# Loading x ahead of the states, and compacting batch 2's x on GpSimd, at the start of a fused attention and maxout kernel

## The chip, the cores and the metric

One core of one Trainium2 chip. The metric is the device time of one execution in microseconds, outputs checked against the reference. Ratios are the mean time of one kernel's fast runs over that of the other's in the same rounds, so they differ a little from the ratio of the medians quoted. Short names: PE is TensorE, ACT is ScalarE, DVE is VectorE, POOL is GpSimd, SP is the engine that issues nearly all DMAs.

## The reference

```python
# x: (8 batches, 8 heads, 512, 64); state: (8, 8, 32, 64); w1, w2: (512, 1024); w_out: (1024, 512)
a     = softmax(x @ state.T / 8);   xread = a @ state
a2    = softmax(state @ x.T / 8);   sread = a2 @ x
y     = concat([xread, sread], axis=2)          # then heads side by side: 4352 x 512
out   = maximum(y @ w1, y @ w2) @ w_out
```

The kernel writes the maximum as relu(y (W1 - W2)) + y W2, so that it needs `wcat` = [W1 - W2 | W2 Wo] beside Wo, and multiplies the small state matrices by `wcat` once per batch (`u_sw`) instead of every row of xread. The result, copied ("evicted") from PSUM to SBUF by ACT and DVE, is `swt`; `l1` multiplies the attention by it, and the relu of that is `r`.

## The kernel before

One in-order program per engine. Weights are prepared while they are loaded; then batch 0 runs, interleaved with the start of batch 1; from batch 1 on a loop repeats, with PE as its bound. Each batch needs its x three ways: as f32 (`xf`), packed to bf16 (`xc`), from which a DMA makes the transpose `xt` that the scores (`u_exp`) read, and padded (`xp`), for the products that give sread. The parts that the change touches (cuts are marked):

```python
    load_states(first)                      # SP's program, in order
    load_x(0, 2)
    # ... W2, Wo in parts
    load_w(w1f, moe_w1, 0)                  # W1a: columns 0 to 511, 1 MB
    load_w(w1f, moe_w1, 1)                  # W1b
    load_states(second)                     # batches 1, 2
    load_x(1)
    load_states(rest)                       # batches 3 to 7
    load_x(2)
    # ...
    for e, i in (("V", slice(0, 2)), ("A", slice(2, 3)), ("P", slice(3, 4))):
        copy(e, w1b[:, i, 0:512], w1f[:, i, 0:512])        # V is DVE, A is ACT, P is POOL
    # ... last products of W2 Wo, their evictions
    u_sw(0, 0)
    u_sw(0, 2)
    w_sub(0); w_sub(1)                      # W1a - W2a on POOL
    l1(0, {}, range(0, 4))
    w_sub(2, nc.vector); w_sub(3, nc.vector)   # W1b - W2b on DVE
    compact_x(1, 0); compact_x(1, 1)        # xc of batch 1, on ACT
    d_xt(1)                                 # SP: transpose of xc into xt
    cast_states("P", second)
    cast_states("P", rest)
    cast_x(1)                               # xp of batch 1, on POOL
    load_x(3)
    sT = d_states(rest)
    # ... batch 0's output products, states(second) on PE, u_sw(0, 1), l1(0, 4..7), u_sw(1, 0)
    u_exp(1, 0); u_exp(1, 1)                # scores of batch 1: read xt
    # ...
    l2_close(0, 1)
    compact_x(2, 0); compact_x(2, 1)        # xc of batch 2, on ACT, one buffer for all batches
    d_xt(2)
    # ... the rest of batch 0, then the loop; in it u_exp(2, ...)
```

The softmax here doesn't subtract the row's maximum and nothing guards it: scores larger than these inputs give would overflow.

## Time and profile before

| | before |
|---|---|
| time, median | 151.57 us (151.40 to 151.83) |
| span of the profiled execution | 149.5 us |
| PE busy | 140.1 us, 94% |
| DMA's share of the chain that ended last | 16% |
| waits of PE for `xt`, batches 1 and 2, in brackets | 0.80 and 0.66 us |

The page's busy shares say that PE is the bound on average; they do not say where a microsecond can be had. That takes the chain in order of time and PE's own timeline, which the prediction shows. A timeline line is start, duration, engine, line, operation, count, and in brackets the idle time of the engine before it and what ended it.

The transpose of the states keeps SP for 4.55 us. Batch 2's `xt` is issued only at 40.62, when ACT has packed its x.

### The profile page before, as it was taken

To read this page: it belongs to the slowest core of one execution; us is meant where nothing else is said; L and a number is where in the kernel's file an instruction comes from. 1 tells how busy PE (TensorE), PEld (TensorE's weight loads), DVE (VectorE), ACT (ScalarE), POOL (GpSimd) and SP (SyncE) were. 2 spreads that over 40 slices of the span, in tenths; PEclk is the share of its full clock that TensorE was granted. 3 is DMA by queue.
4 is the path that set the end of the run, shared out by engine and by line. 5 is a ranking of instruction groups with operands and counts; after the bars stand their busy time and mean duration, and the time that the engine had idled before them with its cause. 6 is when DMAs were issued, how large, how long until landed. Compare 5 with 4: busy or idle time off the path is not lost.

```text
span 149.5 us, 2995 instructions
## 1 busy us (share of the span) xinstructions
PE 140.1 (94%) x1228; PEld 67.7 (45%) x1249; DVE 81.7 (55%) x150; ACT 74.9 (50%) x126; POOL 45.3 (30%) x47
## 2 busy tenths in 40 slices
PE   6988989997989999999999999999999999999991
PEld 2454633434435445444543454445445434664460
DVE  5338628967887097716754582658067725731120
ACT  3166437546877157626844683478157136521010
POOL 3144349880943330550064017104100500000000
PEclk9999999999999999999999999999999999999999
DMA  3999999989989967973979397851556030502423
GB/s 68 381 386 386 388 380 329 301 159 196 214 175 292 324 125 250 313 149 67 302 261 203 116 299 213 158 226 57 105 110 281 0 75 35 245 0 70 136 95 126
DMA packets 37966, 29.89 MB, mean 200 GB/s; under 512 B 24896, under 2 KB 33344, under 8 KB 37056
## 3 DMA queue, kind: packets, MB, share of 16 engines
q1 hardware_dynamic: 37808, 29.56, 69.5%
q8 instruction: 10, 0.16, 0.4%
q10 hardware_dynamic: 144, 0.13, 0.3%
q14 instruction: 4, 0.03, 0.1%
HBM read 15.20 MB, written 8.91 MB: 161 GB/s over the span
## 4 chain that ended last, share of the span: by engine, by line
PE 73%; DMA 16%; SPq 3%; DVE 2%; issue 2%; ACT 2%
PE acc L322 33%; PE ps L307 15%; DMA w1f<-in_moe_w_dram 10%; PE acc L318 9%; DMA xt<-xc 6%; PE ps L279 2%; PE ps L215 2%; PE ps L366 2%; PE acc L376 2%; SPq L98 2%; PE ps L238 2%; PE acc L356 1%; ACT xc L61 1%; PE acc L374 1%; PE acc L279 1%
## 5 line engine op out<-in xcount | busy, mean ns | idle before, releaser
L322 PE MATMUL acc<-wo,r 128*128 128x512 bf16 x238 | 58.3, 379 | 0.5
L322 PEld LDWEIGHTS <-r 128*128 128x128 bf16 x248 | 23.9, 98 | 28.3 <-issue 0.2
L225 POOL TENSOR_TENSOR a<-e,er 128x512 bf16<-128x512 bf16 x14 | 14.4, 1050 | 54.8 <-ACT e L218 39.1
L297 DVE TENSOR_SCALAR r<-ps 128x512 bf16<-128x512 f32 x32 | 22.1, 692 | 13.6 <-PE ps L307 13.6
L307 PE MATMUL ps<-aT,swt 128*128 128x512 bf16 x127 | 29.1, 379 | 0.3 <-DVE swt L63 0.3
L63 DVE COPY ob<-acc 128x512 f32<-128x512 f32 (+1 forms) x17 | 11.1, 655 | 30.2 <-PE acc L322 29.8
L61 ACT COPY ob<-acc 128x512 f32<-128x512 f32 (+1 forms) x16 | 9.2, 574 | 28.6 <-PE acc L322 21.0
L295 ACT ACTIVATE r<-ps 128x512 bf16<-128x512 f32 x32 | 19.2, 602 | 5.9 <-PE ps L307 5.3
L307 PEld LDWEIGHTS <-swt 128*128 128x128 bf16 x128 | 12.1, 98 | 14.9 <-DVE swt L63 0.9
L318 PE MATMUL acc<-swt,aT 128*128 128x512 bf16 x56 | 16.7, 380 | 0.8 <-issue 0.8
L65 POOL CAST xp<-xf 128x2048 bf16<-128x2048 f32 (+1 forms) x8 | 14.1, 1762 | 9.6 <-DMA xf<-in_x_dram 9.6
L61 ACT CAST swt<-ps 128x512 bf16<-128x512 f32 x18 | 9.9, 588 | 13.8 <-PE ps L279 13.8
L61 ACT CAST xc<-xf 128x1024 bf16<-128x1024 f32 x14 | 13.9, 1050 | 1.7 <-DMA xf<-in_x_dram 1.7
L222 DVE TENSOR_REDUCE es<-e 128x16 f32<-128x512 bf16 x16 | 10.6, 659 | 5.0 <-ACT e L218 5.0
L63 DVE CAST swt<-ps 128x512 bf16<-128x512 f32 x18 | 11.6, 679 | 0.9 <-PE ps L279 0.9
L130 PE MATMUL ps<-warm 128*128 128x512 bf16 x24 | 8.7, 493 | 1.3 <-POOL warm L116 1.3
L218 ACT ACTIVATE e<-ps 128x512 bf16<-128x512 f32 x16 | 8.8, 595 | 2.1 <-PE ps L215 1.5
L411 PE MATMUL acc<-wo,w2t 128*128 128x512 bf16 x30 | 7.3, 379 | 0.1
L318 PEld LDWEIGHTS <-aT 128*128 128x128 bf16 x62 | 4.7, 97 | 6.0 <-issue 2.6
L215 PE MATMUL ps<-sbd,xt 128*128 128x64 bf16 x128 | 5.2, 193 | 2.0 <-DMA xt<-xc 1.5
L215 PEld LDWEIGHTS <-xt 128*128 128x128 bf16 x128 | 4.6, 98 | 4.4 <-DMA xt<-xc 2.3
L279 PE MATMUL ps<-wcat,sbd 64*32 64x512 bf16 x136 | 6.3, 382 | 0.0
(73 smaller groups left out, 116.0 us busy)
## 6 DMA issues: line engine op xcount, KB each, us to landing
xf<-in_x_dram SPq DMA_DIRECT2D x7, 1024.0 KB, 7.6
out_dram<-ob SPq DMA_DIRECT2D x7, 1024.0 KB, 5.0
w2f<-in_moe_w_dram SPq DMA_DIRECT2D x2, 1024.0 KB, 9.1
wof<-in_moe_w_out_dram SPq DMA_DIRECT2D x4, 512.0 KB, 10.3
w1f<-in_moe_w_dram SPq DMA_DIRECT2D x2, 1024.0 KB, 15.5
xf<-in_x_dram SPq DMA_DIRECT2D x2, 512.0 KB, 4.5
out_dram<-ob SPq DMA_DIRECT2D x3, 256.0 KB, 2.2
out_dram<-obs SPq DMA_DIRECT2D x8, 64.0 KB, 1.7
```

The lines of the kernel that those rows point to most:

```text
L61: nc.scalar.copy(o, i)
L63: nc.vector.tensor_copy(o, i)
L65: nc.gpsimd.tensor_copy(o, i)
L215: nc.tensor.matmul(p[:, k * 64:k * 64 + 64], d["xt"][:, 4 * i + 2 * g + cp, :], sbd[:, b, 2 * i + g].rearrange("p u n -> p (u n)"), start= ...
L222: nc.vector.tensor_reduce(d["es"][:, g], d["e"][:, g].rearrange("p i c n -> p (i c) n"), axis=mybir.AxisListType.X, op=ALU.add)
L225: mul.tensor_mul(d["a"][:, g].rearrange("p c i n -> p i c n"), d["e"][:, g], d["er"][:, g].rearrange("p (i c) -> p i c", i=4).unsqueeze(3) ...
L279: nc.tensor.matmul(pg[g][32 * i:32 * i + 32, :], sneg[gs, i, :] if k else sbd[gs, b, 2 * i + g, g, :], w[gs, i, ch * 512:(ch + 1) * 512], ...
L295: nc.scalar.activation(out=o, in_=p, func=ACTF.Relu)
L297: nc.vector.tensor_scalar(o, p, scalar1=0.0, scalar2=None, op0=ALU.max)
L307: nc.tensor.matmul(p, SW[b][:, g, f * 128:(f + 1) * 128], AT[b][:, g, :], start=(g == 0), stop=(g == 1))
L318: nc.tensor.matmul(OB[b][1 + c], AT[b][:, g, c * 128:(c + 1) * 128], SW[b][:, g, FF:WC], start=(g == 0), stop=False)
L322: nc.tensor.matmul(OB[b][1 + c], R[b][:, f, c * 128:(c + 1) * 128], wo[:, f, :], start=False, stop=(f == NF - 1))
```

## The change

It means to have x on the chip earlier: x1 (the x of batch 1) ahead of the states of batches 1 and 2, x2 ahead of the other states, batch 2's packing on an idle engine as soon as x2 has landed, into a second buffer, and W1a in two loads, so that half of its casts is done before the rest lands. To make room for that, batch 1's `xp` cast goes from POOL to ACT, and the cast and transpose of the other states come later.

```diff
-            st[b]["xc"] = at.tile([128, H, NC * D], BF16, tag="xc", bufs=1, name="xc")
+            st[b]["xc"] = at.tile([128, H, NC * D], BF16, tag="xc", name="xc")      # pool's two buffers
...
-    load_w(w1f, moe_w1, 0)
+    load_w(w1f, moe_w1, 0, 2)              # two DMAs of half the rows' blocks
     load_w(w1f, moe_w1, 1)
+    load_x(1)
     load_states(second)
-    load_x(1)
-    load_states(rest)
     load_x(2)
...
-    for e, i in (("V", slice(0, 2)), ("A", slice(2, 3)), ("P", slice(3, 4))):
+    for e, i in (("P", slice(0, 1)), ("A", slice(1, 2)), ("V", slice(2, 3)), ("A", slice(3, 4))):
...
     d_xt(1)
+    load_states(rest)
+    cast_x(1, (("A", slice(0, 4)), ("A", slice(4, 8))))
     cast_states("P", second)
-    cast_states("P", rest)
-    cast_x(1)
+    compact_x(2, 0, "P")
+    compact_x(2, 1, "P")
+    d_xt(2)
     load_x(3)
-    sT = d_states(rest)
...
     u_norm(1, 1, nc.gpsimd)
+    cast_states("P", rest)
+    sT = d_states(rest)
     cast_x(2)
...
     l2_close(0, 1)
-    compact_x(2, 0)
-    compact_x(2, 1)
-    d_xt(2)
```

More of the change, by code (lines that the diff above doesn't have):

```diff
@@ L91, with load_w @@
     wof = stage.tile([128, NF, DM], F32)
-    def load_w(t, w, ch):
+    def load_w(t, w, ch, parts=1):
         cs = slice(ch * 512, (ch + 1) * 512)
-        nc.sync.dma_start(out=t[:, :, cs], in_=w.rearrange("(i p) f -> p i f", p=128)[:, :, cs])
+        for k in range(parts):
+            i = slice(4 * k // parts, 4 * (k + 1) // parts)
+            nc.sync.dma_start(out=t[:, i, cs], in_=w.rearrange("(i p) f -> p i f", p=128)[:, i, cs])
     def load_wo(q):
```

## The prediction

> **What bounds the kernel now.** I read the page of the profile first: who is busy, and the chain that ended last.
>
> ```profile
> PE 140.1 (94%) x1228; PEld 67.7 (45%) x1249; DVE 81.7 (55%) x150; ACT 74.9 (50%) x126; POOL 45.3 (30%) x47
> ...
> PE 73%; DMA 16%; SPq 3%; DVE 2%; issue 2%; ACT 2%
> PE acc L322 33%; PE ps L307 15%; DMA w1f<-in_moe_w_dram 10%; PE acc L318 9%; DMA xt<-xc 6%; PE ps L279 2%; PE ps L215 2%; PE ps L366 2%; PE acc L376 2%; SPq L98 2%; PE ps L238 2%; PE acc L356 1%; ACT xc L61 1%; PE acc L374 1%; PE acc L279 1%
> ```
>
> The tensor engine (PE) is busy for 94% of a 149.5 us span and the chain runs through it for 73%. Only two transfers stand in the chain in bulk: the load of W1 (10%) and the transposes of x (6%). The change aims at both. The chain of waits in order of time places them.
>
> ```profile
> 6.24 15.41 DMA w1f<-in_moe_w_dram
> 21.65 0.02 issue
> 21.68 0.69 DVE w1b L63
> ...
> 30.07 4.78 DMA xt<-xc
> 34.85 0.05 issue
> 34.90 0.66 PE ps L215 x16
> ...
> 38.60 1.99 ACT xc L61 x2
> 40.59 0.03 ACT swt L61
> 40.62 4.30 DMA xt<-xc
> 44.92 0.04 issue
> 44.96 0.64 PE ps L215 x16
> ```
>
> Columns are start, duration, what. After 45.0 us the chain has nothing but PE, with pauses of 0.05 to 0.2 us, so nothing that the change does can gain there. Transposes of batches 1 and 2 are each waited for. But a chain counts the whole transfer, and the price is the idle time of PE, which its timeline shows in brackets.
>
> ```profile
> 22.42 0.86 PE L279 MATMUL ps<-w1b,sbd 64*32 64x512 bf16 x8 [0.35 <-DVE w1b L63]
> 22.90 0.60 PE L279 MATMUL ps<-w2b,sneg 64*32 64x512 bf16 x8
> 23.13 0.88 PE L279 MATMUL ps<-wcat,sbd 64*32 64x512 bf16 x8
> 24.27 1.90 PE L307 MATMUL ps<-aT,swt 128*128 128x512 bf16 x8 [0.26 <-DVE swt L63]
> ...
> 34.90 0.64 PE L215 MATMUL ps<-sbd,xt 128*128 128x64 bf16 x16 [0.80 <-DMA xt<-xc]
> ...
> 44.96 0.64 PE L215 MATMUL ps<-sbd,xt 128*128 128x64 bf16 x16 [0.66 <-DMA xt<-xc]
> ```
>
> Open gaps: 0.35 + 0.26 + 0.80 + 0.66 = 2.07 us. Two hidden ones: eight L279 matmuls take 0.41 us later in the trace (at 30.64) and 0.86 and 0.88 here, some 0.45 us lost each. All of it, about 3.0 us, is 2% of the time: the **ceiling** of this change.
>
> **What the Trainium skill says.** "SBUF — State Buffer", section "Who interferes with whom", says that GpSimd (POOL) and VectorE (DVE) share one pair of ports as an exclusive lock: a DVE copy or cast in a two-port mode, or a DVE instruction with two SBUF inputs, fully blocks a GpSimd read, or is blocked, by who issues first. The trace agrees:
>
> ```profile
> 21.70 1.14 POOL L65 CAST w1b<-w1f 128x512 bf16<-128x512 f32 x1 [1.68 <-DMA w1f<-in_moe_w_dram]
> 22.81 4.67 POOL L385 TENSOR_TENSOR wcat<-w1f,w2f 128x1024 bf16<-128x1024 f32 x2
> 27.42 1.61 POOL L65 CAST s_bf<-s_f 128x512 bf16<-128x512 f32 x1
> ```
>
> 512 elements took 1.61 us beside the DVE subtraction of 26.81 to 30.1, although 1280 took 1.76 and 1024 mostly 1.04. The w1b cast of 512 took 1.14, and ended 0.47 us after the DVE cast that started with it (21.68 + 0.69 = 22.37). "GPSIMD Engine Reference", section "4.1 Engine selection", calls one-input GpSimd work "roughly line-rate". The trace: 1024 elements to bf16 took 1.04 us on POOL and 1.05 on ScalarE (ACT), so moving the compaction costs nothing. "DMA: Bandwidth & Descriptors", section "Why small descriptors are slow (HBM only)", gives 256-byte pieces a fixed cost. States go in such pieces: by the landing records the 320 KB of batches 3 to 7 stood 1.38 us behind batch 1's x (28.03 to 29.41), 237 GB/s, while the 1 MB of W1b took 2.82 us (21.65 to 24.47), 372 GB/s.
>
> **The change part by part.**
>
> *W1a in two.* Wo's last part lands at 18.93 and W1a at 21.65, so the first half should land near 20.3. POOL and ACT are free by then (their casts and copies end at 20.0 and 19.3) and finish slices 0 and 1 before 21.65. Then DVE casts one slice (0.43 by its 512-element casts, was 0.69 for two) to 22.1 and ACT one (0.62) to 22.3. PE finishes its previous matmuls at 22.08. The last slice was ready at 22.84 on POOL, so L279 has its inputs 0.54 us earlier. But wcat needs ACT's two copies (to 23.27) and DVE's two (end 23.57, now near 23.3), so L307 starts near 24.0 instead of 24.27: **0.27 us gained**. POOL's two subtractions start up to 0.7 us earlier.
>
> *Order of loads.* x1 takes 3.06 us and the states of batches 1 and 2 take 0.50 (landings 24.97, 28.03). Swapped: x1 lands at 27.5 instead of 28.03, those states at 28.0 instead of 24.97. x2 loses the 1.38 us of the other states ahead of it: 31.2 instead of 32.55.
>
> *The states now come late.* POOL's cast starts at 28.0, behind DVE's subtractions (to about 29.0), and takes 0.6: ready at 29.6. PE arrives at its transposes (29.46 before) near 29.2: a **new stall of 0.4 us**. In addition ACT, after compacting x1 (27.5 to 29.5), now casts x1 too: 2 x 1.05, to 31.6, and only then evicts its half of swt (to 32.2; was 31.74). The L307 of 31.86 moves to about 32.2, and PE reaches batch 1's scores near 34.2 (34.1 before, when it then waited to 34.90).
>
> *xt of batch 1.* Issued at 29.55 rather than 30.07; 4.3 to 4.8 us to landing gives 33.9 to 34.3. Scores start near 34.25: **0.65 earlier in all**, with the 0.27 above already in it, because this wait swallows PE's small delays.
>
> *xt of batch 2.* Its compaction stood in ACT's program behind an output copy, at 38.6, though x2 had landed at 32.55. Now POOL does it at 31.2 to 33.3, its transpose is issued at 33.3 and lands by 38.5, five microseconds before PE asks (about 43.6). The **0.66 us** go.
>
> *What is put off.* The 320 KB of states, their cast (behind POOL's products, to about 39.6) and transpose come later: that transpose is issued over 4.55 us, 39.6 to 44.2 (33.74 before). Its reader was at 55.0, so it is hidden, but the output of batch 0 and the load of x4 behind it go some 0.7 us later, and batch 3's xt, landed at 56.63 for a use at 58.94, may land near 57.4 for a use at 57.6: **0 to 0.5 us back, I take 0.2**.
>
> Sum: 0.65 + 0.66 - 0.2 = 1.1 us; 151.57 - 1.1 = 150.5.
>
> **Rivals.** (1) *The lock turns on PE's path.* At W1a's landing DVE's slice cast and POOL's subtraction start on the same event. If POOL is first, DVE waits out 2.36 us and u_sw of batch 0 is some 2 us late; batch 1's wait can absorb 0.65 of it and batch 2's gap still closes: about 152.4. Before, DVE was 0.03 us ahead of POOL on that event, so I give this one in seven. (2) *A late state replaces the late x.* If the states land at 29 and the cast meets the subtraction, PE stalls 1.4 us at the state transposes; only batch 2's gap is won: 150.9. For it: POOL, PE and DVE meet in this microsecond. (3) *The delayed queue eats it.* If batch 3's xt or its a-transpose is late by a microsecond, it is 151.3 or no gain. Against it: the slack of 2.3 us. (4) *All goes well*, hidden L279 losses included: 149.5.
>
> **Range and chances.** Two gaps worth 1.3 us are nearly sure to shrink; the rest are exchanges of some tenths. Low 149.7 is nearly all of the gaps; high 152.0 takes in rivals 2 and 3 and part of 1. Faster by 2% (under 148.5) would need 3.0 us, the whole ceiling: 3%. Slower by 2% (over 154.6) would need rival 1 with another stall: 4%. Within: 93%.
>
> **What would show it.** L215's two bracketed waits should be gone or under 0.2 us; xc of batch 2 on POOL near 31 to 33.3; x2's landing near 31.2. A wait of about 0.4 before the state transposes (L154) at 29 to 30 shows the swap's price. L307's first group at 24.0 shows the W1a split; at 26 it shows rival 1, with DVE's w1b cast over 2 us long. A bracketed wait before batch 3's L215 near 57.6 shows rival 3. The prediction is wrong if a wait that I don't have appears on PE after 45 us, or if a POOL cast runs into the products that PE's a-transposes of batch 1 need at 39.2.

## More of the kernel before

One more view is needed later: how SP issued the transposes before. The columns are start, duration of the issue on SP, queue, line, what.

```profile
30.07 3.00 SPq L189 DMA_TRANSPOSE xt<-xc  x1
33.19 0.50 SPq L80 DMA_DIRECT2D xf<-in_x_dram  x1
33.74 4.55 SPq L142 DMA_TRANSPOSE sT<-s_bf  x1
40.62 2.82 SPq L189 DMA_TRANSPOSE xt<-xc  x1
43.55 0.52 SPq L332 DMA_DIRECT2D out_dram<-ob  x1
```

## The result, and the profile after

The changed kernel took **149.73 us** (149.66 to 149.82, 4 runs) against 151.49 for the kernel before in the same rounds: ratio 0.9881, 95% interval 0.9863 to 0.9899. A later set of rounds, `e11` below, gave 149.75 and 0.9898 (0.9882 to 0.9915). So the gain is 1.5 to 1.8 us where 1.1 was forecast.

The page of the kernel after, its chain by engine and line:

```profile
PE 74%; DMA 14%; SPq 7%; ACT 2%; issue 1%
PE acc L323 34%; PE ps L308 16%; DMA xf<-in_x_dram 11%; PE acc L319 8%; SPq L97 4%; DMA xt<-xc 3%; PE ps L280 3%; PE ps L216 2%; PE ps L367 2%; PE acc L377 2%; PE ps L239 2%; SPq L100 2%; PE acc L357 1%; ACT xc L61 1%; PE acc L375 1%
```

`xt` has gone from 6% to 3%: one transpose is left of two. The load of W1 has been replaced by the load of x (`xf`). The chain in order of time, for the kernel after, says which transpose is left:

```profile
11.39 16.16 DMA xf<-in_x_dram
27.57 1.99 ACT xc L61 x2
29.59 4.50 DMA xt<-xc
```

It is batch 1's: x1 lands, ACT packs it, the DMA transposes it, PE starts. PE's timeline after, at the places that the prediction showed for before (lines are one higher than before: L216 was L215):

```profile
23.92 1.90 PE L308 MATMUL ps<-aT,swt 128*128 128x512 bf16 x8 [0.21 <-DVE swt L63]
...
29.34 0.40 PE L155 MATMUL ps<-ident,s_bf 128*128 128x128 bf16 x4
...
33.61 0.41 PE L280 MATMUL ps<-wcat,sbd 64*32 64x512 bf16 x8
34.14 0.71 PE L216 MATMUL ps<-sbd,xt 128*128 128x64 bf16 x16
...
40.01 3.63 PE L308 MATMUL ps<-aT,swt 128*128 128x512 bf16 x16
43.47 0.63 PE L216 MATMUL ps<-sbd,xt 128*128 128x64 bf16 x16
...
57.43 0.63 PE L216 MATMUL ps<-sbd,xt 128*128 128x64 bf16 x16
```

Both bracketed waits are gone, though a little of the first is left: 0.53 us pass from the group ahead of batch 1's scores (33.61 to 34.14), where 0.34 do in `e9` below, whose `xt` is early. So 0.19 us are still waited; before, it was 0.87 (33.69 to 34.90, less 0.34). Set beside before:

| PE comes to | before, us | after, us | earlier by |
|---|---|---|---|
| first group of `l1` of batch 0 | 24.27 | 23.92 | 0.35 |
| scores of batch 1 | 34.90 | 34.14 | 0.76 |
| scores of batch 2 | 44.96 | 43.47 | 1.49 |
| scores of batch 3 | 58.94 | 57.43 | 1.51 |

After batch 2 nothing is won or lost. SP's issues and POOL's work after:

```profile
29.59 1.88 SPq L190 DMA_TRANSPOSE xt<-xc  x1
31.52 1.14 SPq L85 DMA_DIRECT2D s_f<-in_state_dram  x1
33.09 2.75 SPq L190 DMA_TRANSPOSE xt<-xc  x1
35.96 0.51 SPq L80 DMA_DIRECT2D xf<-in_x_dram  x1
39.64 1.51 SPq L143 DMA_TRANSPOSE sT<-s_bf  x1
41.24 1.20 SPq L333 DMA_DIRECT2D out_dram<-ob  x1
```

```profile
21.69 4.90 POOL L386 TENSOR_TENSOR wcat<-w1f,w2f 128x1024 bf16<-128x1024 f32 x2 [0.76 <-DMA w1f<-in_moe_w_dram]
...
28.16 1.13 POOL L65 CAST s_bf<-s_f 128x512 bf16<-128x512 f32 x1 [1.39 <-DMA s_f<-in_state_dram]
31.04 2.03 POOL L65 CAST xc<-xf 128x1024 bf16<-128x1024 f32 x2 [1.75 <-DMA xf<-in_x_dram]
36.36 2.06 POOL L226 TENSOR_TENSOR a<-e,er 128x512 bf16<-128x512 bf16 x2 [3.29 <-DVE er L225]
```

POOL packs batch 2's x at 31.04 in a hole that it had, and its transpose is issued at 33.09 instead of 40.62. The states' transpose, moved from 33.74 to 39.64, now takes 1.51 us to issue, not 4.55, and batch 0's output goes out at 41.24, 2.3 us *earlier* than before.

### The profile page after: what moved, and what is told of

Its sections match the earlier page's. It is cut to its first block, busy times and chain, and to the rows that moved or that the text cites. A ratio compares the mean times of both kernels' runs of the same rounds, so it can differ in the third digit from the quotient of the medians.

```text
span 147.9 us, 3003 instructions
## 1 busy us (share of the span) xinstructions
PE 139.4 (94%) x1228; PEld 67.4 (46%) x1249; DVE 81.7 (55%) x150; ACT 75.7 (51%) x127; POOL 44.2 (30%) x48
## 4 chain that ended last, share of the span: by engine, by line
PE 74%; DMA 14%; SPq 7%; ACT 2%; issue 1%
PE acc L323 34%; PE ps L308 16%; DMA xf<-in_x_dram 11%; PE acc L319 8%; SPq L97 4%; DMA xt<-xc 3%; PE ps L280 3%; PE ps L216 2%; PE ps L367 2%; PE acc L377 2%; PE ps L239 2%; SPq L100 2%; PE acc L357 1%; ACT xc L61 1%; PE acc L375 1%
## 5 line engine op out<-in xcount | busy, mean ns | idle before, releaser
L308 PE MATMUL ps<-aT,swt 128*128 128x512 bf16 x127 | 29.1, 379 | 0.3 <-DVE swt L63 0.2
L308 PEld LDWEIGHTS <-swt 128*128 128x128 bf16 x128 | 12.0, 98 | 15.0 <-DVE swt L63 0.8
L65 POOL CAST xp<-xf 128x2048 bf16<-128x2048 f32 (+1 forms) x7 | 12.2, 1745 | 11.0 <-DMA xf<-in_x_dram 11.0
L61 ACT CAST xc<-xf 128x1024 bf16<-128x1024 f32 x12 | 11.9, 1051 | 1.6 <-DMA xf<-in_x_dram 1.6
L131 PE MATMUL ps<-warm 128*128 128x512 bf16 x24 | 7.7, 444 | 1.3 <-POOL warm L117 1.3
L216 PEld LDWEIGHTS <-xt 128*128 128x128 bf16 x128 | 4.8, 98 | 2.8 <-ACT xt L61 0.8
L216 PE MATMUL ps<-sbd,xt 128*128 128x64 bf16 x128 | 5.3, 193 | 0.7 <-ACT xt L61 0.6
```

The lines of the kernel that those rows point to most:

```text
L61: nc.scalar.copy(o, i)
L65: nc.gpsimd.tensor_copy(o, i)
L216: nc.tensor.matmul(p[:, k * 64:k * 64 + 64], d["xt"][:, 4 * i + 2 * g + cp, :], sbd[:, b, 2 * i + g].rearrange("p u n -> p (u n)"), start= ...
L308: nc.tensor.matmul(p, SW[b][:, g, f * 128:(f + 1) * 128], AT[b][:, g, :], start=(g == 0), stop=(g == 1))
```

## The experiments

Twelve runs in three sets (`e11` is the changed kernel again); those of a set share the runs of the kernel before (medians 151.40, 151.33 and 151.48). "Worth" is one minus the ratio, times that median. All results were correct.

### One part alone

**`e1`: W1a's two loads and its casts, alone.**

```diff
-    load_w(w1f, moe_w1, 0)
+    load_w(w1f, moe_w1, 0, 2)
...    # and the changed kernel's tuple of casts
```

> The kernel before with only W1a's two loads and the new split of its casts. Theory A (the early part is bounded by batch 1's xt, which lands at 34.85 whatever PE does before): L307's first group starts 0.35 us earlier (23.9 instead of 24.27), PE then waits 0.35 us longer for xt, and the time does not move: 0.0 us, within 0.15. Rival B (the parts add up, the split is worth its 0.35 us by itself): 0.3 to 0.4 us faster.

151.36 us, ratio 0.9990 (0.9976 to 1.0005): no gain shown. PE's timeline of `e1`:

```profile
34.90 0.64 PE L217 MATMUL ps<-sbd,xt 128*128 128x64 bf16 x16 [0.96 <-DMA xt<-xc]
```

The bracket has grown from 0.80 to 0.96: PE comes 0.16 us earlier, waits longer and starts at 34.90 as before. A head start ahead of a wait is worth nothing until the wait moves.

**`e2`: batch 2's packing on POOL and its early transpose, alone.**

```diff
     cast_x(1)
+    compact_x(2, 0, "P")
+    compact_x(2, 1, "P")
+    d_xt(2)
     load_x(3)
...    # without compact_x(2, ...), d_xt(2) after l2_close(0, 1); xc with two buffers
```

> The kernel before with only batch 2's compaction on POOL in a second buffer and its transpose issued ahead of the load of x3 and of the states' transpose. Loads as before. Theory A: the wait at batch 2's scores goes, the wait at batch 1's stays; gain 0.7 to 0.85 us, more than the 0.66 us that the bracket showed, because the last matmul's modelled end hides 0.16 us of each wait. Rival B: the bracket is the whole wait: 0.66 us or less.

150.52 us, ratio 0.9933 (0.9919 to 0.9947): worth 1.0 us (0.8 to 1.2), more than the bracket of 0.66. In `e2`'s own trace batch 2's scores start 0.73 us earlier, at 44.23. The traces show why a bracket is too small. In the kernel after, 16 matmuls of L308 start at 40.01 and the next starts at 43.47, 3.46 us later; before, the same group started at 40.69 and the next at 44.96, 4.27 us later:

```profile
40.69 3.61 PE L307 MATMUL ps<-aT,swt 128*128 128x512 bf16 x16
```

The loss is 4.27 - 3.46 = 0.81 us. The bracket leaves 0.16 out, because it counts from the modelled end of the last matmul (379 ns after its start), while the next one can start 216 ns after it (3.46 / 16). The Trainium skill, "TensorE: Matmul & The Clock Gate", sections "Single matmul latency" and "Back-to-back issue gap", gives formulas for these two, the second for a matmul by itself: as estimates, (398 + 512) / 2.4 = 379 ns and 512 / 2.4 + 2.5 = 216 ns. The starts of these sixteen, each with a weight load, agree with 216. The 379 is no second measurement: the profile models where a matmul ends.

**`e3`: the order of loads alone**, with batch 2 packed late by ACT in one buffer, and the other states' cast and transpose late.

```diff
-    load_states(second)
     load_x(1)
-    load_states(rest)
+    load_states(second)
     load_x(2)
...
     d_xt(1)
+    load_states(rest)
...    # cast_states("P", rest) after u_norm(1, 1); d_states(rest) after d_xt(2)
```

> The kernel before with only the order of loads changed (x1, states of batches 1 and 2, x2, the other states later; their cast and transpose later, too, as they must be). Batch 2 is compacted by ACT late and in one buffer, as before. Theory A: x1 lands near 27.5 and x2 near 31.0, xt of batch 1 near 34.1, so 0.6 to 0.75 us is gained there, and the wait of 0.66 at batch 2 stays: 0.6 to 0.8 us faster. Rival B (the earlier x only helps together with the split, since PE is not there earlier): 0.4 or less.

151.03 us, ratio 0.9964 (0.9950 to 0.9978): worth 0.55 us (0.3 to 0.8), between the theories by the interval. PE's timeline of `e3`:

```profile
33.74 0.90 PE L214 MATMUL ps<-sbd,xt 128*128 128x64 bf16 x16
...
44.43 0.64 PE L214 MATMUL ps<-sbd,xt 128*128 128x64 bf16 x16 [1.03 <-DMA xt<-xc]
```

Batch 1's scores start 1.2 us earlier, 0.3 of that because this whole execution ran ahead (its `l1` began at 23.98, not 24.27). At batch 2 the bracket has grown from 0.66 to 1.03 and takes a part back. My expectation that this wait would stay at 0.66 was wrong: ACT's packing moved with PE, its transpose took 4.66 us to land instead of 4.30.

**`e4`: the changed kernel with W1a whole.**

```diff
-    load_w(w1f, moe_w1, 0, 2)
+    load_w(w1f, moe_w1, 0)
...    # and before's tuple of casts
```

> The changed kernel with W1a in one load and the casts split as before. Theory A: PE comes to batch 1's scores 0.35 us later than in the changed kernel, of which about 0.2 is hidden behind xt's landing at 34.1: 0.1 to 0.25 us slower than the changed kernel, 1.5 to 1.7 faster than before. Rival B (parts add up): 0.35 us or more slower than the changed kernel.

149.83 us, ratio 0.9891 (0.9875 to 0.9907): 1.65 us faster than before, against 1.5 to 1.8 for the changed kernel. The split's own share, about 0.1 us by the medians, cannot be told from zero.

### What each part needs

**`e5`: the lock.** DVE's cast of W1a's slice 2 in two halves.

```diff
-        copy(e, w1b[:, i, 0:512], w1f[:, i, 0:512])
+        for h in (slice(0, 256), slice(256, 512)) if e == "V" else (slice(0, 512),):
+            copy(e, w1b[:, i, h], w1f[:, i, h])
```

> The changed kernel with DVE's cast of W1a's slice 2 in two halves of 256 columns, so that POOL's first subtraction, which starts on the same landing, can come in between. Theory A (exclusive lock on the shared port pair, won by who issues first): the first half ends near 21.95, POOL then holds the pair for 2.36 us, the second half ends near 24.4 instead of 22.1; L308's first group starts near 26.1 instead of 23.9, batch 1's scores near 36.2 instead of 34.1, and the time is 1.8 to 2.2 us longer than the changed kernel's (149.7), about 151.6. Rival B (the ports are shared, or DVE keeps them between two of its instructions): 0.0 to 0.3 us longer.

152.28 us median, ratio 1.0070 (1.0016 to 1.0124): slower than the kernel before. The four executions are 151.59, 151.60, 152.95 and 153.25. DVE's and PE's timelines of the slowest of them:

```profile
21.64 2.64 DVE L63 CAST w1b<-w1f 128x256 bf16<-128x256 f32 x2 [3.10 <-DMA w1f<-in_moe_w_dram]
```

```profile
24.34 0.40 PE L280 MATMUL ps<-w1b,sbd 64*32 64x512 bf16 x4 [2.08 <-DVE w1b L63]
...
26.14 3.50 PE L308 MATMUL ps<-aT,swt 128*128 128x512 bf16 x8 [0.21 <-DVE swt L63]
```

And POOL's:

```profile
21.69 4.80 POOL L386 TENSOR_TENSOR wcat<-w1f,w2f 128x1024 bf16<-128x1024 f32 x2 [0.76 <-DMA w1f<-in_moe_w_dram]
```

Two casts that should take half a microsecond take 2.64: POOL's first subtraction, 2.4 us long (4.80 for two), stands between them. Theory A holds, and rival 1 of the prediction was real, just not taken: in the changed kernel, with one cast, DVE started at 21.64 and POOL at 21.69. DVE was the first in all 14 traces, by 0.03 us (where POOL starts with a cast) or 0.05. The two fast executions lie at 151.6 as expected. The other two have a mean granted clock of 0.989. Busy time in windows for `e5` (window, its length, busy us of PE, PEld, DVE, ACT and POOL, then PE's granted clock, DMA share, GB/s):

```profile
24.00:26.00 2.00, 1.39 (x20) 0.32 (x19) 2.00 (x4) 0.61 (x2) 2.00 (x2) 1.00 1.15 324
26.00:28.00 2.00, 1.86 (x5) 0.73 (x6) 0.68 (x2) 1.16 (x2) 0.68 (x2) 0.50 1.10 334
28.00:30.00 2.00, 2.00 (x8) 0.74 (x6) 1.01 (x2) 1.09 (x2) 0.61 (x1) 0.65 0.54 167
```

After PE's pause its clock is halved for 3.4 us (26.0 to 29.4 in the clock records), and `l1`'s eight matmuls take 3.50 us instead of 1.90. I had not expected that. That the pause did it is argued from the order in time: of the four executions this one alone is traced, and the two of 151.6 us, the same program, kept the whole clock.

**`e6`: batch 2's packing on ACT**, at the same place.

```diff
-    compact_x(2, 0, "P")
-    compact_x(2, 1, "P")
+    compact_x(2, 0, "A")
+    compact_x(2, 1, "A")
```

> The changed kernel with batch 2's compaction on ACT instead of POOL, at the same place of the program. Theory A (what counts is not that x2 is compacted early but that an engine off PE's path does it): ACT, whose program is in order, compacts x1, casts x1, compacts x2 (31.5 to 33.4) and only then evicts its half of swt, so L308's second group starts near 33.9 instead of 31.8 and the time is 1.7 to 2.1 us longer than the changed kernel's. Rival B (ACT has room, the engine doesn't matter): within 0.3 us of the changed kernel.

151.53 us, ratio 1.0015 (1.0000 to 1.0030): the whole gain is lost. PE's timeline of `e6`:

```profile
31.90 0.39 PE L308 MATMUL ps<-aT,swt 128*128 128x512 bf16 x1
33.89 1.69 PE L308 MATMUL ps<-aT,swt 128*128 128x512 bf16 x7 [1.60 <-ACT swt L61]
```

ACT packs until 33.3 and only then evicts the `swt` that PE needs. The work is the same (1.99 us on ACT, 2.03 on POOL, for two instructions); what gains is that the engine is not on PE's path.

**`e7`: one buffer for `xc`.**

```diff
-            st[b]["xc"] = at.tile([128, H, NC * D], BF16, tag="xc", name="xc")
+            st[b]["xc"] = at.tile([128, H, NC * D], BF16, tag="xc", bufs=1, name="xc")
```

> The changed kernel with one buffer for the compacted x instead of two. Theory A (the second buffer is not what gains): POOL's compaction of x2 waits for batch 1's transpose (34.1) and ends near 36.2, xt of batch 2 lands near 40.9, still 2.5 us ahead of its use at 43.5: within 0.2 us of the changed kernel. Rival B (the second buffer is needed): 0.5 us or more slower.

149.67 us, ratio 0.9908 (0.9881 to 0.9936): by the median as fast as the changed kernel (one of four executions took 150.38). Packing waits for batch 1's transpose and runs from 33.91; `xt` of batch 2 lands at 42.20 by the landing records, later than the 40.9 expected, and PE asks at 43.22. The second buffer gains nothing.

**`e12`: the other states ahead of x2 again.**

```diff
     load_states(second)
+    load_states(rest)
     load_x(2)
...
     d_xt(1)
-    load_states(rest)
```

> The changed kernel with the states of batches 3 to 7 loaded ahead of x2, as before, and not after the first transpose. Theory A (of the order of loads only x1's place gains; x2 has slack): x2 lands near 32.4 instead of 31.0, xt of batch 2 near 39.2 instead of 37.9, still 4 us ahead of its use: within 0.15 us of the changed kernel. Rival B (x2's earlier landing is part of the gain, by batch 2's transpose or by what batch 1's transpose meets in the queue): 0.3 us or more slower.

149.82 us, ratio 0.9896 (0.9882 to 0.9909), beside 149.75 and 0.9898 for the changed kernel in the same set. Of the order of loads, x2's place is worth nothing that can be told from zero; with `e3`, that leaves x1's, which was not run by itself.

### The changed kernel again, and versions meant to beat it

**`e11`: the changed kernel, unaltered.**

> The changed kernel itself, unaltered, beside the others on one chip, as the measure for them and for the size of the gain. From the traces PE comes to batch 2's scores 1.49 us earlier and the span is 1.6 shorter: 1.5 to 1.8 us faster than before.

149.75 us, ratio 0.9898: worth 1.5 us (1.3 to 1.8).

**`e8`: x1 and those states ahead of W1b, too.**

```diff
-    load_w(w1f, moe_w1, 1)
     load_x(1)
     load_states(second)
+    load_w(w1f, moe_w1, 1)
     load_x(2)
```

> The changed kernel with x1 and the states of batches 1 and 2 loaded ahead of W1b as well. Theory A (what is left of PE's waits before 35 us hangs on x1 and those states): x1 lands near 24.7, its compaction starts when ACT has done its second relu (26.0), xt lands near 32.7, the state transposes wait for nothing, and PE comes to batch 1's scores near 33.8: 0.2 to 0.4 us faster than the changed kernel. W1b lands near 28.0, and DVE's subtractions (2.35) end at 30.4, just before L280 reads them at 30.5. Rival B (that subtraction is then late and takes the place of the wait): within 0.1 us or slower.

149.84 us, ratio 0.9905 (0.9890 to 0.9920): rival B. W1b lands at 27.89, DVE's subtractions end at 30.3 and its copies of the states, the next in its program, at 31.0, so its half of `swt` comes late: `l1`'s second group starts at 31.82, as it did in the changed kernel (31.76). One wait took the place of another.

**`e9`: W1b in two quarters of columns**, one ahead of x1 and one behind those states.

```diff
-    load_w(w1f, moe_w1, 1)
+    load_w1q(2)                            # columns 512 to 767
     load_x(1)
     load_states(second)
+    load_w1q(3)
     load_x(2)
```

> The changed kernel with W1b in two loads of 256 columns, the first ahead of x1 and the states of batches 1 and 2, the second behind them. In e8 DVE's two subtractions waited for all of W1b (27.9) and their end (30.2) took the place of the old waits; here the first can run near 26.5 and the second near 27.9, ending near 29.0. Theory A: no wait before L280 at 30.1 or L308 at 31.5, xt of batch 1 lands near 33.0, and PE comes to batch 1's scores near 33.7 instead of 34.1: 0.3 to 0.5 us faster than the changed kernel. Rival B: 1 KB pieces or the late swt of ACT eat it: within 0.15.

149.58 us, ratio 0.9881 (0.9867 to 0.9894), against 149.75 and 0.9898 for the changed kernel beside it: 0.17 us by the medians, but the intervals overlap. The waits are gone; PE's timeline of `e9`:

```profile
33.48 0.41 PE L285 MATMUL ps<-wcat,sbd 64*32 64x512 bf16 x8
33.82 0.90 PE L221 MATMUL ps<-sbd,xt 128*128 128x64 bf16 x16
34.78 0.81 PE L328 MATMUL acc<-wo,r 128*128 128x512 bf16 x3
```

Scores start 0.34 us after the group before them, its own pace. But from there to L328 it now takes 0.96 us (0.69 before, 34.90 to 35.59), so half of the 0.32 us won at batch 1 (33.82 against 34.14 in `e11`) is given back within a microsecond. The trace shows what PE waits for there. The eighth of the sixteen score matmuls starts at 34.04 and the ninth only at 34.33, and by the semaphore events of the trace the ninth was released by this instruction of DVE, a relu of the `l1` group ahead:

```profile
33.59 0.69 DVE L303 TENSOR_SCALAR r<-ps 128x512 bf16<-128x512 f32 x1 [0.17 <-PE ps L313]
```

It ends at 34.28. So with `xt` early, DVE's relu, which reads a `ps` tile in PSUM, binds next; no run varied it.

**`e10`: `e9` with the evictions of W2 Wo spread.**

```diff
+        if i.start == 2:
+            copy("A", wcat[:, 0, FF:WC], WO[0])
         copy(e, w1b[:, i, 0:512], w1f[:, i, 0:512])
+    copy("A", wcat[:, 1, FF:WC], WO[1])
+    copy("V", wcat[:, 2, FF:WC], WO[2])
+    copy("V", wcat[:, 3, FF:FF + 256], WO[3][:, 0:256])
+    copy("A", wcat[:, 3, FF + 256:WC], WO[3][:, 256:512])
...    # in place of w_wo_out(0) to (3)
```

> The run above, with the four evictions of W2 x Wo spread so that ACT does the first before its last w1b cast and the last is shared: wcat is ready near 23.1 instead of 23.3, L308's first group starts near 23.7 instead of 23.9, and nothing later binds: 0.15 to 0.25 us faster than the run above. Rival B: another wait takes the place: within 0.1.

149.71 us, ratio 0.9885 (0.9867 to 0.9904): no gain. ACT's timeline of `e10`:

```profile
23.32 0.37 ACT L61 CAST wcat<-acc 128x256 bf16<-128x256 f32 x1 [0.29 <-DVE wcat L63]
```

The two halves of the last eviction, meant to run side by side, ran one after the other: ACT waited for DVE's half. `e9` has the lowest median of all; that it beats the changed kernel is not shown.

## Why the prediction was right or wrong

Its account of what gains held: both waits for `xt` went. Its sum did not: it forecast 1.1 us and 1.5 to 1.8 came, so the center of 150.5 was 0.8 us too slow and 149.73 lies at the low end of the range. The step that failed is "What is put off": it took 0.2 us back for a delayed queue, and the queue was not delayed (nothing was given back: 1.49 us at batch 2, 1.51 at batch 3). Two more terms were too small: batch 1's `xt` (0.65 us for a measured 0.76) and batch 2's (0.66 for 0.73).

- **"W1a in two", 0.27 us.** PE's first `l1` group came 0.35 us earlier. Right, too, that the wait for `xt` swallows it: alone it gave nothing (`e1`).
- **"Order of loads".** x1 landed at 27.55 for 27.5 forecast, the states at 28.10 for 28.0, x2 at 30.99 for 31.2.
- **"The states now come late".** The new stall of 0.4 us is 0.23: the transposes start 1.96 us after the output group ahead of them (27.38 to 29.34), and 1.73 before (27.73 to 29.46). ACT's `swt` half ended at 31.94, not 32.2, and the second `l1` group started at 31.76, 0.1 earlier than before and not 0.34 later. None of it cost time, since batch 1's `xt` came last, but the forecast of the next step was built on it.
- **"xt of batch 1", 0.65 us.** Mis-sized: 0.76. Issue (29.59 for 29.55) and landing (34.10, in the middle of 33.9 to 34.3) came as forecast. What was off is PE's arrival: I had PE reach the scores near 34.2, behind a late `swt`. The group ahead started at 33.61, so at its own pace of 0.34 us PE was there at 33.95, and the landing alone set the start at 34.14.
- **"xt of batch 2", "The 0.66 us go".** Mis-sized, and this is an error of reading: I took the bracket for the loss. The wait cost 0.81 us, and the stretch between batch 1's and batch 2's scores shrank from 10.06 to 9.33, by 0.73. Alone the part was worth 0.8 to 1.2 us (`e2`).
- **"What is put off", "0 to 0.5 us back, I take 0.2".** The step that failed outright: nothing was given back, and batch 0's output went earlier, not later. It carried the 4.55 us issue of the states' transpose over to its new place. That issue followed one of the 1 MB load of x3 by 0.05 us; in its new place, 3.2 us behind that load's issue, it took 1.51. And it overlooked what batch 2's late transpose had held up on SP, which is in order: before, the last copy of batch 0's output was done at 41.83, and the output was issued at 43.55, behind the 2.82 us issue of that `xt`. After, the copy is done at 41.15 and the output goes at 41.24: 2.3 us earlier, where 0.7 later was forecast. Batch 3's `xt` landed at 55.09 (56.63 before) for a use at 57.43: the slack of 2.3 us is whole. That the load just ahead of the transpose set its issue time is argued from these two places and from other runs: in `e2` it took 4.39 us, 0.06 us behind that load, though it came 4.5 us later than before; in `e7` 3.61 when 0.4 behind, in `e11` 1.75 when 3.0 behind. A transpose of x still under way does not make it long: in `e3` one was, and it took 1.56. No run varied the place by itself, and why it takes so long stays open.

Corrected, the sum is 0.76 + 0.73 + 0 = 1.49 us at batch 2's scores, which is what PE's timeline shows. `e11` agrees with it; the first set's 1.8 us (1.5 to 2.1) is 0.3 more at its center. Nothing in the trace accounts for that, and the two executions that were profiled are 1.6 us apart (151.30 and 149.72).

Rival 1 was rightly kept: `e5` made it happen. One in seven looks too much: DVE is first in all 14 traces. Its price was put at 152.4: two executions of `e5` took 151.6, and two 153.0 and 153.3, in which the clock added some 1.5 us. Of rival 2 a little came: POOL's cast met DVE's subtraction and took 1.13 us (0.61 in `e8`, where it met none), which goes with the stall of 0.23. Rival 3 did not occur. Rival 4's 149.5 is nearer to the result than the center is, but not by the hidden losses that it counts in: of the two, one went (0.86 to 0.45 us), one stayed (0.88 and 0.91), and batch 1's wait swallows both.

Of the things in the change, two do the work: x1 ahead of the first states, and batch 2's packing by an engine with a hole. Neither the second buffer (`e7`), nor x2's place (`e12`), nor the split of W1a (`e1`, `e4`) has a worth that can be told from zero. The move of batch 1's `xp` cast to ACT was not run alone; `e2` and `e3`, which leave it on POOL, add up to 1.55 us, as much as the whole change in `e11`, so nothing points to a gain from it.

## What to carry to other kernels

Measure a stall of PE as the distance from start to start less the same group's pace elsewhere; the idle time in a bracket leaves out part of it, 0.16 us at batch 2 here and 0.07 at batch 1. When a step is moved, take its issue time from where it will stand in the queue, and ask what its old place was holding up: taking a late item out of an in-order queue frees everything behind it. And let a change of several parts be run one part at a time, since a head start in front of a wait shows nothing and the parts that carry the gain can be fewer than the parts of the change.

## What the Trainium skill lacked or had wrong

- "TensorE: Matmul & The Clock Gate", section "Why this matters for your kernels", warns of pauses of PE longer than about 3 us. In `e5`'s trace a pause of 2.08 us by the bracket, with two of 0.20 and 0.21 us in the two microseconds behind it, was followed by half clock for 3.4 us; a second of its four executions has the same mean clock (0.989), two have 1.000. One of 1.60 us (`e6`) was not, in four (mean clock 0.996 or more). So a pause shorter than the page's was not safe here each time; where the limit lies, no run shows.
- "SBUF — State Buffer", section "Who interferes with whom", is borne out: POOL's subtraction took the pair for its whole length between two DVE casts (2.64 us for the two), and DVE's two subtractions took 2.35 us where no POOL cast came between them (3.29 before, where one did). What it lacks is who wins when both are released by one DMA: DVE did, by 0.03 to 0.05 us, in all 14 traces.
- "DMA: Bandwidth & Descriptors", section "DMA Transpose (X-bar)", has no word on how long such a transpose holds the issuing engine; elsewhere the page has sequencer times by size alone. Here, over all runs, one of the same size took 1.33 to 4.55 us on SP (the states'), and 1.82 to 3.06 (batch 1's `xt`).
